# Factor tiles of 128 columns instead of 98 in an agent-attention kernel with an expert pass

## The chip, the cores and the metric

The kernel runs on one core of a Trainium2 chip. The core has TensorE (PE, the matrix array of 128 rows and 128 columns; its weight loads, PEld, run beside its matmuls), VectorE (DVE), ScalarE (ACT), GpSimd (POOL), and DMA queues, of which the one issued by SyncE (SP) carries nearly all of the data. The metric is the device time of one execution in microseconds (us); lower is better. TensorE runs at a granted clock of 2.4 GHz (written 1.00 in the profile) or 1.2 GHz (0.50).

## What is computed

Four batches (B = 4), N = 12608 tokens of C = 128 features, 49 agents for each batch. Agents attend to keys and values, tokens attend to agents, and then the 128 tokens of each batch with the highest gate score go through an expert of two layers with 1024 hidden features:

```
def sm(a, b):
    s = scale * (a @ b.transpose(0, 2, 1))
    s = s - s.max(-1, keepdims=True)
    e = np.exp(s)
    return e / (e.sum(-1, keepdims=True) + 1e-09)
a2k = sm(agents, k)
agent_v = a2k @ v
q2a = sm(q, agents)
out = q2a @ agent_v
# then, for each batch b, with x = out
scores = np.einsum('bsd,d->bs', x, w_gate)
top_idx = np.argpartition(-scores[b], capacity)[:capacity]   # capacity = 128
h = np.maximum(x[b, top_idx] @ w1, 0.0)
out[b, top_idx] = x[b, top_idx] + 1/(1+exp(-scores)) * (h @ w2)
```

## The kernel before, in words

Each batch's tokens are cut into seven chunks, six of 15 tiles and one of 9 tiles of 128 tokens. For each chunk the kernel does the following.

- `k_front` and `q_scores` load a transposed chunk of keys or queries (`xT`) and form the scores `S` with the agents on TensorE; VectorE turns them into tiles `sk` (keys) and `sq` (queries) with the tokens on the partitions, 49 used columns for each tile of tokens.
- `k_exp` and `q_exp` subtract a maximum (GpSimd) and take the exponential (ScalarE).
- `v_tiles` multiplies the key weights with the values into `av` (TensorE, 128 rows by 64 columns of the array, float32); `v_finish` makes of it the float16 matrix `ws` (`d["W"]`), 98 rows, which holds a high and a low half of the agent values, their gate scores, and a column of ones.
- `q_high` and `q_low` write the **factor tile** `f`: for each tile of tokens 98 float16 columns, 49 with the high half of the exponential (ScalarE) and 49 with the low half (GpSimd). The ring of `f` has two buffers (`N_F`).
- `q_turn` transposes `f` on TensorE (98 rows of `fT` in PSUM, eight tiles of tokens in one group) and copies the result to `ft` (ScalarE, a few on VectorE).
- `q_gate` multiplies each transposed tile `ft`, as the weights, with the three gate columns of `ws` (`pg`, 3 moving columns); `q_rates` and `topk` make the scores and the choice of the 128 tokens from it. In `topk` the tile `all` is a broadcast of candidates by TensorE, and VectorE (`ge`) and ScalarE (`ga`) take turns in counting on it.
- `q_out` multiplies each `ft` tile, as the weights, with the high and then the low half of `ws` (`po`, 128 moving columns each); `po` is copied and scaled to `og` by VectorE, ScalarE or ScalarE and GpSimd, and stored.
- `expert` gathers the chosen tokens' queries (`xq`), forms their output again in float32 (`sc`, `e`, `eT`, `xT`, `xe`), and runs the two layers (`ph`, `py`). It runs for batches 0 to 2 together and then for batch 3 alone.

Nothing is issued in the order of the code. A recorder collects all instructions, and a planner (`place`) lays them out once, engine by engine, by hand-set urgencies (`RANKS`), by data dependences, by free buffers, and by a price for each instruction. The price of an instruction counts its columns and the elements of one partition, not the number of partitions. The kernel then issues that order (line 1220), so that each engine works through its own list strictly in sequence. The outputs of batches 1, 3 and 2 (`TAIL`) come late in TensorE's list, with the experts among them.

Of the kernel before, what the change touches and what calls it, by code (L numbers as in the profile page):

```python
# [15 lines left out]
F16 = mybir.dt.float16  # L16
# [4 lines left out]
ALU = mybir.AluOpType  # L21
# [3 lines left out]
P = 128  # L25
# [3 lines left out]
A = 49  # L29
# [4 lines left out]
TMAX = max(CHUNKS)  # L34
# [10 lines left out]
N_F = 2  # L45
# [446 lines left out]
def agent_attention_moe(ctx, tc, qT, kT, va, agT, wgb, w1, w2, consts, qs, outs, capacity):  # L492
    nc = rec = Recorder(tc.nc)
    rec.tag = ("setup", 0)
    B = len(outs)
    C = qT.shape[1]
# [10 lines left out]
    qp = rec.pool(ctx.enter_context(tc.tile_pool(name="qp", bufs=2)), "qp", 2)  # L507
    sm = rec.pool(ctx.enter_context(tc.tile_pool(name="sm", bufs=2)), "sm", 2)
# [35 lines left out]
    def cs(name):  # L544
        return cst[:, spot[name][0]:spot[name][1]]
# [3 lines left out]
    idh = const.tile([P, P], F16, name="idh")  # L549
# [28 lines left out]
    def scores(src, b, c, dst, top=None):  # L578
# [4 lines left out]
        for h in range(2):  # L583
# [85 lines left out]
    def v_finish(b):  # L669
        d = st[b]  # L670
        R = 2 * A
        a = sm.tile([P, C + 1], F32, tag="avs", name=f"avs_{b}", bufs=1)
        nc.vector.tensor_copy(a, d["av"][:, :C + 1])
        pw = psT.tile([P, 512], F32, tag="T", name=f"pw_{b}")
        nc.tensor.matmul(pw[:R, :C + 1], cs("sel"), a, start=True, stop=True)
        yield
        wf = d["wf"] = wfs[:, b]
        rs = sm.tile([R, 1], F32, tag="rs", name=f"rs_{b}", bufs=1)
        nc.vector.tensor_scalar(rs, pw[:R, C:C + 1], 1e-9, None, op0=ALU.add)
        nc.vector.reciprocal(rs, rs)  # L680
# [13 lines left out]
        nc.vector.tensor_scalar(
            iv[:, 1:2].bitcast(I32), iv[:, 0:1].bitcast(I32), -1.0, float((254 + WEXP) << 23),
            op0=ALU.mult, op1=ALU.add,
        )
        up = iv[:R, 1:2]
        ws = sm.tile([R, 3, C + 1], F16, tag="ws", name=f"ws_{b}", bufs=B)
        nc.gpsimd.memset(ws[:, 2, C:], 1.0)  # L700
        nc.vector.tensor_scalar(ws[:, 0, :C], pw[:R, :C], rs, up, op0=ALU.mult, op1=ALU.mult)
        g2 = sm.tile([R, 2], F32, tag="g2", name=f"g2_{b}", bufs=1)
        nc.scalar.mul(g2[:, 0:1], rs, up)
        nc.scalar.mul(g2[:, 1:2], wf[:, C:C + 1], up)
        nc.vector.scalar_tensor_tensor(
            ws[:, 1, :C], pw[:R, :C], g2[:, 0:1], ws[:, 0, :C], op0=ALU.mult, op1=ALU.subtract
        )
        nc.scalar.copy(ws[:, 0, C:], g2[:, 1:2])
        nc.gpsimd.tensor_tensor(ws[:, 1, C:], g2[:, 1:2], ws[:, 0, C:], op=ALU.subtract)
        nc.scalar.mul(iv[:, 0:1], iv[:, 0:1], 2.0 ** -WEXP / FSCALE)  # L710
        d["W"] = ws
        d["iv"] = iv
        yield
# [24 lines left out]
    def q_high(b, c):  # L738
        n = CHUNKS[c]
        d = st[b]  # L740
        sv = d["q", c][:, :n, :A]
        if b in EARLY:
            nc.gpsimd.tensor_tensor(
                sv, sv, d["qm", c][:, :n].unsqueeze(2).broadcast_to([P, n, A]), op=ALU.mult
            )
        f = qp.tile([P, TMAX, 2 * A], F16, tag="f", name=f"f_{b}_{c}", bufs=N_F)
        d["f", c] = f
        copy = {"A": nc.scalar.copy, "P": nc.gpsimd.tensor_copy, "V": nc.vector.tensor_copy}[HI[b]]
        copy(f[:, :n, :A], d["q", c][:, :n, :A])

    def q_low(b, c):
        n = CHUNKS[c]
        f = st[b]["f", c]
        nc.gpsimd.tensor_tensor(
            f[:, :n, A:], st[b]["q", c][:, :n, :A], f[:, :n, :A], op=ALU.subtract
        )

    def q_turn(b, c, t0):
        n = CHUNKS[c]
        d = st[b]  # L760
        nt = min(8, n - t0)
        if nt <= 0:
            return
        f = d["f", c]
        if t0 == 0:
            ring, tag, w = (skp, "sk", TMAX) if b == B - 1 and FT_LAST == "sk" else (ftp, "ft", TMAX)
            if tag == "ft" and c == NCH - 1:
                tag, w = "fs", n
            ft = ring.tile([P, w, AP_], F32, tag=tag, name=f"ft_{b}_{c}", bufs={"sk": N_SK, "ft": N_FT, "fs": B - 1}[tag])
            d["ft", c] = ft.rearrange("p t a -> p (t a)").bitcast(F16)  # L770
        pt = psT.tile([P, 1024], F16, tag="T", name=f"fT_{b}_{c}_{t0}")
        with rec.group():
            for t in range(nt):
                turn = nc.tensor.transpose(pt[:2 * A, P * t:P * t + P], f[:, t0 + t, :], idh)
        if b == B - 1:
            turn.deps.add(d["mb_set"].seq)
        (nc.vector.tensor_copy if TURN[b][t0 // 8] == "V" else nc.scalar.copy)(
            d["ft", c][:2 * A, P * t0:P * (t0 + nt)], pt[:2 * A, :P * nt]
        )

    def q_tile(b, c, t):
        return st[b]["ft", c][:2 * A, P * t:P * t + P]

    def q_gate(b, c):

# [29 lines left out]
    def q_out(b, c, t0):  # L815
# [351 lines left out]
    for b in range(B):  # L1167
# [14 lines left out]
        with rec.at("fin", b):  # L1182
            run(v_finish(b))
        for c in range(NCH):
            with rec.at("q", b, c):
                q_scores(b, c)
            with rec.at("qe", b, c):
                q_exp(b, c)
                q_high(b, c)
                q_low(b, c)  # L1190
            with rec.at("turn", b, c):
                for t0 in range(0, CHUNKS[c], 8):
                    q_turn(b, c, t0)
            with rec.at("gate", b, c):
                q_gate(b, c)
# [103 lines left out]
```

## Time and profile before

| | |
|---|---|
| time, median of 3 runs | 319.38 us (317.65 to 322.01) |
| the profiled execution | 318.6 us |
| its span, first to last instruction | 316.7 us |
| PE busy | 281.7 us, 89% of the span |
| PEld busy | 189.2 us, 60% |
| DVE busy | 225.5 us, 71% |
| POOL busy | 179.9 us, 57% |
| ACT busy | 170.8 us, 54% |
| HBM | 79.87 MB read, 26.21 MB written |
| mean granted clock of TensorE | 0.959 |

The profile comes from one execution. "Busy" is the time in which an engine executes something. PE's matmuls are pipelined, so the durations of neighbouring matmuls overlap; how fast a group of them goes is read from the length of the group, less the length of one, over the number of steps. The granted clock is listed for any stretch of the span. A releaser, "<-DVE og", is what ended an engine's idle time. All times within the span are counted from its first instruction.

### The profile page before, as it was taken

To read this page: it belongs to the slowest core of one execution; us is meant where nothing else is said; L and a number is where in the kernel's file an instruction comes from. 1 tells how busy PE (TensorE), PEld (TensorE's weight loads), DVE (VectorE), ACT (ScalarE), POOL (GpSimd) and SP (SyncE) were. 2 spreads that over 40 slices of the span, in tenths; PEclk is the share of its full clock that TensorE was granted. 3 is DMA by queue.
4 is the path that set the end of the run, shared out by engine and by line. 5 is a ranking of instruction groups with operands and counts; after the bars stand their busy time and mean duration, and the time that the engine had idled before them with its cause. 6 is when DMAs were issued, how large, how long until landed. Compare 5 with 4: busy or idle time off the path is not lost. (4 is left out here: it accounts for less than half of the span.)

```text
span 316.7 us, 8554 instructions
## 1 busy us (share of the span) xinstructions
PE 281.7 (89%) x3524; PEld 189.2 (60%) x3524; DVE 225.5 (71%) x507; ACT 170.8 (54%) x306; POOL 179.9 (57%) x152
## 2 busy tenths in 40 slices
PE   2789879999999999999899998799988969799993
PEld 0133426456335555667664556587978969799593
DVE  0899885797978858658798867848366937769630
ACT  1036645645674533754963666878278835824320
POOL 1046399867869715337723859975245744655232
PEclk9999999999999999999999999999797996958998
DMA  7999999999999999999999997997631893876650
GB/s 291 414 414 419 419 413 416 415 418 418 415 414 407 416 420 332 419 421 386 394 368 402 417 400 281 339 350 210 237 126 58 337 364 128 357 291 261 248 209 31
DMA packets 18203, 106.69 MB, mean 337 GB/s; under 512 B 2032, under 2 KB 3440, under 8 KB 18160
## 3 DMA queue, kind: packets, MB, share of 16 engines
q1 hardware_dynamic: 17472, 105.07, 83.8%
q8 instruction: 30, 0.49, 0.6%
q0 software_dynamic: 256, 0.52, 0.5%
q10 hardware_dynamic: 432, 0.50, 0.4%
q14 instruction: 13, 0.11, 0.1%
HBM read 79.87 MB, written 26.21 MB: 335 GB/s over the span
## 5 line engine op out<-in xcount | busy, mean ns | idle before, releaser
L1220 PE MATMUL S<-xT,ag_sb 128*32 128x480 f32 (+1 forms) x896 | 101.7, 561 | 15.0 <-DMA ag_sb<-agT 6.2
L1220 POOL TENSOR_TENSOR sq<-sq,qm 128x735 f32<-128x735 f32 (+1 forms) x35 | 47.5, 1365 | 54.3 <-DVE qm L1220 51.2
L1220 PEld LDWEIGHTS <-ft 98*128 98x128 f16 x1188 | 65.6, 104 | 15.4 <-issue 13.9
L1220 PE MATMUL po<-ws,ft 98*128 98x128 f16 x792 | 61.9, 236 | 2.8 <-DVE og L1220 1.8
L1220 POOL TENSOR_TENSOR og<-og,r 128x512 f32<-128x512 f32 (+1 forms) x39 | 36.2, 943 | 41.1 <-ACT og L1220 40.9
L1220 PE MATMUL av<-v,sk 128*64 128x129 f32 x792 | 55.5, 283 | 2.8 <-DVE avs L1220 1.3
L1220 PEld LDWEIGHTS S<-xT,ag_sb 128*32 128x32 f32 x896 | 24.0, 110 | 53.9 <-issue 18.8
L1220 PEld LDWEIGHTS av<-v,sk 128*64 128x64 f32 x792 | 47.3, 139 | 14.0 <-issue 6.0
L1220 ACT COPY ft<-fT 98x896 f16<-98x896 f16 (+2 forms) x49 | 43.1, 897 | 23.1 <-PE fT L1220 19.8
L1220 POOL TENSOR_TENSOR f<-sq,f 128x735 f16<-128x735 f32 (+1 forms) x28 | 41.1, 1472 | 19.6 <-ACT f L1220 13.7
L1220 POOL TENSOR_TENSOR sk<-sk,mb 128x735 f32<-128x735 f32 (+1 forms) x28 | 46.8, 1700 | 7.4 <-DVE mb L1220 7.3
L1220 DVE STREAM_TRANSPOSE sq<-S 128x480 f32<-128x480 f32 (+1 forms) x56 | 35.2, 641 | 10.7 <-PE S L1220 10.0
L1220 ACT ACTIVATE sq<-sq,lift 128x735 f32<-128x735 f32 (+1 forms) x28 | 24.6, 887 | 30.1 <-POOL sq L1220 30.1
L1220 DVE TENSOR_REDUCE mx<-S 128x1 f32<-128x480 f32 (+1 forms) x56 | 33.0, 612 | 9.0 <-PE S L1220 8.6
L1220 DVE STREAM_TRANSPOSE sk<-S 128x480 f32<-128x480 f32 (+1 forms) x56 | 34.8, 637 | 4.9 <-PE av L1220 3.1
L1220 PEld LDWEIGHTS <-f 128*98 128x98 f16 x396 | 24.7, 124 | 20.7 <-issue 10.1
L1220 DVE SCALAR_TENSOR_TENSOR ge<-all,top,minus 128x512 bf16<-128x512 f32 x32 | 24.0, 750 | 14.8 <-ACT ga L1220 9.2
L1220 DVE TENSOR_REDUCE qm<-sq 128x15 f32<-128x735 f32 (+1 forms) x35 | 30.3, 867 | 2.4 <-ACT sq L1220 1.6
L1220 PE MATMUL fT<-idh,f 128*98 128x128 f16 x396 | 29.6, 222 | 2.6 <-POOL f L1220 1.0
L1220 DVE TENSOR_TENSOR og<-po,r 128x512 f32<-128x512 f32 (+1 forms) x42 | 26.9, 657 | 5.8 <-PE po L1220 1.9
L1220 ACT ACTIVATE sk<-sk 128x735 f32<-128x735 f32 (+1 forms) x28 | 22.1, 794 | 16.2 <-POOL sk L1220 16.1
L1220 ACT ACTIVATE ga<-all,top 128x512 bf16<-128x512 f32 x32 | 22.0, 687 | 12.2 <-DVE ge L1220 11.5
(130 smaller groups left out, 234.8 us busy)
## 6 DMA issues: line engine op xcount, KB each, us to landing
v<-va SPq DMA_DIRECT2D x24, 967.5 KB, 7.9
xT<-kT SPq DMA_DIRECT2D x24, 960.0 KB, 8.2
xT<-qT SPq DMA_DIRECT2D x24, 960.0 KB, 9.4
out<-og SPq DMA_DIRECT2D x24, 960.0 KB, 4.1
v<-va SPq DMA_DIRECT2D x4, 580.5 KB, 8.5
xT<-kT SPq DMA_DIRECT2D x4, 576.0 KB, 8.4
xT<-qT SPq DMA_DIRECT2D x4, 576.0 KB, 9.7
out<-og SPq DMA_DIRECT2D x4, 576.0 KB
```

Of the source, the lines that this page charges most:

```text
L1220: call(*args, **kwargs)
```

## The change

The factor tiles get 128 columns (`P`) instead of 98 (`2 * A`). The 30 added columns are zero: both buffers of the ring are cleared once, by two GpSimd memsets ahead of the loop, and nothing writes these columns later. The transposes then use 128 columns of the array and give 128 rows of `fT`; the copies to `ft` move 128 partitions; the gates and the outputs use 128 rows as weights. `ws` gets 128 rows as well, whose rows 98 to 127 are cleared by a GpSimd memset for each batch.

```
--- before.py
+++ after.py
@@ -598,6 +598,9 @@
             if top is not None:
                 nc.vector.tensor_reduce(top[:, h:h + 1], ps[:, :w], axis=AX.X, op=ALU.max)
 
+    for i in range(N_F):
+        f = qp.tile([P, TMAX, P], F16, tag="f", name=f"f0_{i}", bufs=N_F)
+        nc.gpsimd.memset(f, 0.0)
     st = [{} for _ in range(B)]
     tail, filled, turns = set(), set(), []
     OUT_PS = ((psO, "O"), (psS, "S"), (psS, "S"), (psS, "S"))
@@ -696,17 +699,18 @@
             op0=ALU.mult, op1=ALU.add,
         )
         up = iv[:R, 1:2]
-        ws = sm.tile([R, 3, C + 1], F16, tag="ws", name=f"ws_{b}", bufs=B)
-        nc.gpsimd.memset(ws[:, 2, C:], 1.0)
-        nc.vector.tensor_scalar(ws[:, 0, :C], pw[:R, :C], rs, up, op0=ALU.mult, op1=ALU.mult)
+        ws = sm.tile([P, 3, C + 1], F16, tag="ws", name=f"ws_{b}", bufs=B)
+        nc.gpsimd.memset(ws[96:], 0.0)
+        nc.gpsimd.memset(ws[:R, 2, C:], 1.0)
+        nc.vector.tensor_scalar(ws[:R, 0, :C], pw[:R, :C], rs, up, op0=ALU.mult, op1=ALU.mult)
         g2 = sm.tile([R, 2], F32, tag="g2", name=f"g2_{b}", bufs=1)
         nc.scalar.mul(g2[:, 0:1], rs, up)
         nc.scalar.mul(g2[:, 1:2], wf[:, C:C + 1], up)
         nc.vector.scalar_tensor_tensor(
-            ws[:, 1, :C], pw[:R, :C], g2[:, 0:1], ws[:, 0, :C], op0=ALU.mult, op1=ALU.subtract
-        )
-        nc.scalar.copy(ws[:, 0, C:], g2[:, 1:2])
-        nc.gpsimd.tensor_tensor(ws[:, 1, C:], g2[:, 1:2], ws[:, 0, C:], op=ALU.subtract)
+            ws[:R, 1, :C], pw[:R, :C], g2[:, 0:1], ws[:R, 0, :C], op0=ALU.mult, op1=ALU.subtract
+        )
+        nc.scalar.copy(ws[:R, 0, C:], g2[:, 1:2])
+        nc.gpsimd.tensor_tensor(ws[:R, 1, C:], g2[:, 1:2], ws[:R, 0, C:], op=ALU.subtract)
         nc.scalar.mul(iv[:, 0:1], iv[:, 0:1], 2.0 ** -WEXP / FSCALE)
         d["W"] = ws
         d["iv"] = iv
@@ -743,7 +747,7 @@
             nc.gpsimd.tensor_tensor(
                 sv, sv, d["qm", c][:, :n].unsqueeze(2).broadcast_to([P, n, A]), op=ALU.mult
             )
-        f = qp.tile([P, TMAX, 2 * A], F16, tag="f", name=f"f_{b}_{c}", bufs=N_F)
+        f = qp.tile([P, TMAX, P], F16, tag="f", name=f"f_{b}_{c}", bufs=N_F)
         d["f", c] = f
         copy = {"A": nc.scalar.copy, "P": nc.gpsimd.tensor_copy, "V": nc.vector.tensor_copy}[HI[b]]
         copy(f[:, :n, :A], d["q", c][:, :n, :A])
@@ -752,7 +756,7 @@
         n = CHUNKS[c]
         f = st[b]["f", c]
         nc.gpsimd.tensor_tensor(
-            f[:, :n, A:], st[b]["q", c][:, :n, :A], f[:, :n, :A], op=ALU.subtract
+            f[:, :n, A:2 * A], st[b]["q", c][:, :n, :A], f[:, :n, :A], op=ALU.subtract
         )
 
     def q_turn(b, c, t0):
@@ -771,15 +775,15 @@
         pt = psT.tile([P, 1024], F16, tag="T", name=f"fT_{b}_{c}_{t0}")
         with rec.group():
             for t in range(nt):
-                turn = nc.tensor.transpose(pt[:2 * A, P * t:P * t + P], f[:, t0 + t, :], idh)
+                turn = nc.tensor.transpose(pt[:, P * t:P * t + P], f[:, t0 + t, :], idh)
         if b == B - 1:
             turn.deps.add(d["mb_set"].seq)
         (nc.vector.tensor_copy if TURN[b][t0 // 8] == "V" else nc.scalar.copy)(
-            d["ft", c][:2 * A, P * t0:P * (t0 + nt)], pt[:2 * A, :P * nt]
+            d["ft", c][:, P * t0:P * (t0 + nt)], pt[:, :P * nt]
         )
 
     def q_tile(b, c, t):
-        return st[b]["ft", c][:2 * A, P * t:P * t + P]
+        return st[b]["ft", c][:, P * t:P * t + P]
 
     def q_gate(b, c):
 
```

GpSimd's list at the start of the program, before (`ws_0` to `ws_3` are the ones of the four batches, `idf` is the float32 identity, of which VectorE makes the float16 identity of the transposes; `sq_2_6` is the queries' last chunk of batch 2, the first real work):

```order
L1220 MEMSET ws_1_290 98x1
L1220 MEMSET ws_2_423 98x1
L1220 MEMSET idf_96 128x128
L1220 MEMSET ws_0_158 98x1
L1220 MEMSET ws_3_556 98x1
L1220 ISA
L1220 AFFINE_SELECT idf_96<-idf_96 128x128
L1220 TENSOR_TENSOR sq_2_6_480<-sq_2_6_480,qm_2_6_484 128x9x49
```

The same place of GpSimd's list now (`f0_0` and `f0_1` are the two buffers of the factor tiles):

```order
L1224 MEMSET ws_1_292 32x387
L1224 MEMSET ws_2_425 32x387
L1224 MEMSET idf_96 128x128
L1224 MEMSET ws_1_292 98x1
L1224 MEMSET ws_2_425 98x1
L1224 MEMSET f0_0_109 128x1920
L1224 MEMSET f0_1_110 128x1920
L1224 ISA
L1224 AFFINE_SELECT idf_96<-idf_96 128x128
L1224 MEMSET ws_0_160 32x387
L1224 MEMSET ws_3_558 32x387
L1224 TENSOR_TENSOR sq_2_6_482<-sq_2_6_482,qm_2_6_486 128x9x49
```

Four of the six added memsets stand ahead of the identity's last step (AFFINE_SELECT), and all six ahead of the first real work. (Two one-column memsets of `ws` that stand before the last row are not shown.)

TensorE's list at the end of the gates of batch 2, before (about 225 to 234 us of the span; `av_3` are the key-value products of batch 3, `all0_2` the broadcast that opens the choice of tokens of batch 2):

```order
L1220 LDWEIGHTS ft_2_1_441
L1220 MATMUL pg_2_434<-ws_2_423,ft_2_1_441 128x3
L1220 MATMUL av_3_543<-v_3_3_546,sk_3_3_520 64x129 x15
L1220 MATMUL av_3_543<-v_3_4_547,sk_3_4_524 64x129 x15
L1220 LDWEIGHTS f_3_6_618
L1220 MATMUL fT_3_6_8_621<-idh_97,f_3_6_618 98x128
L1220 MATMUL all0_2_494<-idf_96,top_2_490 128x128 x4
L1220 MATMUL av_3_543<-v_3_5_548,sk_3_5_528 64x129 x15
```

The same place now:

```order
L1224 LDWEIGHTS ft_2_1_443
L1224 MATMUL pg_2_436<-ws_2_425,ft_2_1_443 128x3
L1224 MATMUL av_3_545<-v_3_3_548,sk_3_3_522 64x129 x15
L1224 MATMUL av_3_545<-v_3_4_549,sk_3_4_526 64x129 x15
L1224 LDWEIGHTS f_3_6_620
L1224 MATMUL fT_3_6_8_623<-idh_97,f_3_6_620 128x128
L1224 MATMUL all0_2_496<-idf_96,top_2_492 128x128 x4
L1224 MATMUL av_3_545<-v_3_5_550,sk_3_5_530 64x129 x15
```

Nothing has moved here; the transpose has 128 output rows instead of 98. The same holds for all of TensorE's, VectorE's, ScalarE's and SyncE's lists: the same instructions in the same order with the same waits, wider where they touch `f`, `fT`, `ft` or `ws`. GpSimd's list differs only at its start.

## Rows read from the trace of the kernel before

**Rows 1.** The page: busy time by engine, and two lines of the 40 slices.

```profile
PE 281.7 (89%) x3524; PEld 189.2 (60%) x3524; DVE 225.5 (71%) x507; ACT 170.8 (54%) x306; POOL 179.9 (57%) x152
PEclk9999999999999999999999999999797996958998
DMA  7999999999999999999999997997631893876650
```

**Rows 2.** Groups by line and shape: busy us, mean ns of one, idle before.

```profile
L1220 PEld LDWEIGHTS <-ft 98*128 98x128 f16 x1188 | 65.6, 104 | 15.4 <-issue 13.9
L1220 PEld LDWEIGHTS <-f 128*98 128x98 f16 x396 | 24.7, 124 | 20.7 <-issue 10.1 <-POOL f L1220 9.0 <-POOL sq L1220 1.6
L1220 PE MATMUL po<-ws,ft 98*128 98x128 f16 x792 | 61.9, 236 | 2.8 <-DVE og L1220 1.8 <-ACT og L1220 0.9
L1220 PE MATMUL fT<-idh,f 128*98 128x128 f16 x396 | 29.6, 222 | 2.6 <-POOL f L1220 1.0 <-POOL sq L1220 0.6 <-DVE m L1220 0.4
L1220 PE MATMUL pg<-ws,ft 98*128 98x3 f16 x396 | 12.3, 167 | 0.3 <-issue 0.3
L1220 POOL TENSOR_TENSOR sk<-sk,mb 128x735 f32<-128x735 f32 x24 | 42.5, 1793 | 7.4 <-DVE mb L1220 7.3
```

**Rows 3.** PE's timeline at full clock: start us, length us, group.

```profile
130.25 1.00 PE L1220 MATMUL fT<-idh,f 128*98 128x128 f16 x15
131.19 0.61 PE L1220 MATMUL po<-ws,ft 98*128 98x128 f16 x8
131.64 0.94 PE L1220 MATMUL pg<-ws,ft 98*128 98x3 f16 x30
232.00 1.97 PE L1220 MATMUL av<-v,sk 128*64 128x129 f32 x30
```

**Rows 4.** Stretches: length, busy us (instructions) by engine, PEclk, DMA share, GB/s.

```profile
222.50:225.90 3.40, 3.40 (x101) 3.38 (x100) 0.04 (x1) 0.93 (x1) 1.25 (x1) 1.00 0.94 295
225.90:229.30 3.40, 3.40 (x34) 3.40 (x34) 2.28 (x8) 0.38 (x1) 0.00 (x0) 0.50 0.56 228
273.70:277.10 3.40, 1.99 (x27) 1.62 (x25) 2.35 (x7) 2.85 (x7) 1.71 (x3) 1.00 1.00 407
277.10:280.50 3.40, 3.02 (x32) 3.01 (x31) 2.54 (x10) 1.08 (x4) 1.98 (x3) 0.50 0.67 276
280.50:287.30 6.80, 6.80 (x61) 6.80 (x60) 4.85 (x15) 2.46 (x5) 4.35 (x5) 0.50 0.87 348
287.30:290.70 3.40, 3.40 (x61) 3.39 (x59) 3.37 (x8) 1.63 (x5) 0.89 (x2) 1.00 0.83 313
```

**Rows 5.** PE's timeline, 223 to 231 us.

```profile
223.67 2.15 PE L1220 MATMUL pg<-ws,ft 98*128 98x3 f16 x75
225.75 5.19 PE L1220 MATMUL av<-v,sk 128*64 128x129 f32 x60
```

**Rows 6.** PE's waits, 236 to 317 us: us in total, times, longest.

```profile
PE all L1220 <- ACT ga L1220: 2.3, 1, 2.3
```

**Rows 7.** PE's timeline, 281 to 290 us.

```profile
281.79 1.46 PE L1220 MATMUL sc<-ag_sb,xT 128*128 128x49 f32 x6
...
283.11 5.96 PE L1220 MATMUL po<-ws,ft 98*128 98x128 f16 x68
288.90 0.49 PE L1220 MATMUL eT<-idf,e 128*49 128x128 f32 x3
```

**Rows 8.** VectorE's timeline at the start of the program.

```profile
9.25 0.23 DVE L1220 CAST tri_b<-cst 128x128 bf16<-128x128 f32 x1 [7.58 <-DMA cst<-consts]
```

**Rows 9.** GpSimd's timeline at the start of the program.

```profile
0.80 0.21 POOL L1220 MEMSET idf<- 128x128 f32 x1
...
1.12 0.29 POOL L1220 TENSOR_SCALAR_AFFINE_SELECT idf<-idf 128x128 f32<-128x128 f32 x1
17.57 0.93 POOL L1220 TENSOR_TENSOR sq<-sq,qm 128x441 f32<-128x441 f32 x1 [16.16 <-DVE qm L1220]
```

**Rows 10.** The chain that ended last: shares of the span by engine and line.

```profile
by line: PE po L1220 4.4%; PE py L1220 2.3%; PE ph L1220 2.0%; PE sc L1220 0.4%; PE xT L1220 0.4%; DVE og L1220 0.4%; PE xe L1220 0.3%; DVE g L1220 0.3%; issue 0.3%; POOL out L1220 0.2%; ACT og L1220 0.2%; POOLq L1225 0.2%; DVE hT L1220 0.1
```

More of the change, by code (lines that the diff above doesn't have):

```diff
@@ L599, in scores @@
                 nc.vector.tensor_reduce(top[:, h:h + 1], ps[:, :w], axis=AX.X, op=ALU.max)
+    for i in range(N_F):
+        f = qp.tile([P, TMAX, P], F16, tag="f", name=f"f0_{i}", bufs=N_F)
+        nc.gpsimd.memset(f, 0.0)
     st = [{} for _ in range(B)]
@@ L698, in v_finish @@
         up = iv[:R, 1:2]
-        ws = sm.tile([R, 3, C + 1], F16, tag="ws", name=f"ws_{b}", bufs=B)
-        nc.gpsimd.memset(ws[:, 2, C:], 1.0)
-        nc.vector.tensor_scalar(ws[:, 0, :C], pw[:R, :C], rs, up, op0=ALU.mult, op1=ALU.mult)
+        ws = sm.tile([P, 3, C + 1], F16, tag="ws", name=f"ws_{b}", bufs=B)
+        nc.gpsimd.memset(ws[96:], 0.0)
+        nc.gpsimd.memset(ws[:R, 2, C:], 1.0)
+        nc.vector.tensor_scalar(ws[:R, 0, :C], pw[:R, :C], rs, up, op0=ALU.mult, op1=ALU.mult)
         g2 = sm.tile([R, 2], F32, tag="g2", name=f"g2_{b}", bufs=1)
@@ L705, in v_finish @@
         nc.vector.scalar_tensor_tensor(
-            ws[:, 1, :C], pw[:R, :C], g2[:, 0:1], ws[:, 0, :C], op0=ALU.mult, op1=ALU.subtract
+            ws[:R, 1, :C], pw[:R, :C], g2[:, 0:1], ws[:R, 0, :C], op0=ALU.mult, op1=ALU.subtract
         )
-        nc.scalar.copy(ws[:, 0, C:], g2[:, 1:2])
-        nc.gpsimd.tensor_tensor(ws[:, 1, C:], g2[:, 1:2], ws[:, 0, C:], op=ALU.subtract)
+        nc.scalar.copy(ws[:R, 0, C:], g2[:, 1:2])
+        nc.gpsimd.tensor_tensor(ws[:R, 1, C:], g2[:, 1:2], ws[:R, 0, C:], op=ALU.subtract)
         nc.scalar.mul(iv[:, 0:1], iv[:, 0:1], 2.0 ** -WEXP / FSCALE)
@@ L745, in q_high @@
             )
-        f = qp.tile([P, TMAX, 2 * A], F16, tag="f", name=f"f_{b}_{c}", bufs=N_F)
+        f = qp.tile([P, TMAX, P], F16, tag="f", name=f"f_{b}_{c}", bufs=N_F)
         d["f", c] = f
@@ L754, in q_low @@
         nc.gpsimd.tensor_tensor(
-            f[:, :n, A:], st[b]["q", c][:, :n, :A], f[:, :n, :A], op=ALU.subtract
+            f[:, :n, A:2 * A], st[b]["q", c][:, :n, :A], f[:, :n, :A], op=ALU.subtract
         )
@@ L773, in q_turn @@
             for t in range(nt):
-                turn = nc.tensor.transpose(pt[:2 * A, P * t:P * t + P], f[:, t0 + t, :], idh)
+                turn = nc.tensor.transpose(pt[:, P * t:P * t + P], f[:, t0 + t, :], idh)
         if b == B - 1:
@@ L777, in q_turn @@
         (nc.vector.tensor_copy if TURN[b][t0 // 8] == "V" else nc.scalar.copy)(
-            d["ft", c][:2 * A, P * t0:P * (t0 + nt)], pt[:2 * A, :P * nt]
+            d["ft", c][:, P * t0:P * (t0 + nt)], pt[:, :P * nt]
         )
     def q_tile(b, c, t):
-        return st[b]["ft", c][:2 * A, P * t:P * t + P]
+        return st[b]["ft", c][:, P * t:P * t + P]
     def q_gate(b, c):
```

## The prediction

> **What bounds the kernel now.** The page is read first [rows 1]. Its two lines of slices show two stages. Up to slice 28 (some 222 us) the DMA engines are busy in seven tenths or more of every slice, nine tenths or more in nearly all, and TensorE's clock is at full rate; after that the DMA digits vary between 0 and 9, and in the same slices the clock falls for the first time (digits down to 5). In the first stage a faster TensorE brings little, since the loads do not come faster. In the second stage the loads are over. There the chain that ended last [rows 10] is followed back from the last instruction, and it lies on TensorE: the outputs po 4.4%, the expert's py 2.3% and ph 2.0%, and only tenths of a per cent on other engines.
>
> Next come the groups by shape, for what the change widens [rows 2]: 396 transposes, 396 gates, 792 outputs, and as many weight loads. Their mean durations (222, 167 and 236 ns) say little, since neighbours overlap. The pace is read from the timeline at full clock [rows 3]: 15 transposes take 1.00 us, so (1.00 − 0.22)/14 = 56 ns a step; 8 outputs (0.61 − 0.24)/7 = 53 ns; 30 gates (0.94 − 0.17)/29 = 27 ns. Gates and outputs load the same weights (98 rows, 128 columns), and the gates show that such a load goes through every 27 ns. So the outputs are paced by their 128 moving columns, not by the load, and the transposes run at the same pace with loads of 98 columns.
>
> Last come stretches of the second stage, for the clock [rows 4]. In 222.5 to 225.9 us TensorE is busy all the time, mostly with 75 gates of 3 moving columns [rows 5], and in the next stretch, to 229.3, the clock is 0.50. In 273.7 to 277.1 it is busy for 1.99 of 3.40 us, and the clock is 0.50 from 277.1 to 287.3, though TensorE is busy for 3.02 of the first 3.40 and for all of the next 6.80 us. At 287.3 it is back at 1.00.
>
> **The change part by part.**
>
> *Transposes, gates, outputs at one clock: 0.* The moving columns are the same (128, 3, 128), and the numbers of instructions too. A step of 56, 27 or 53 ns is set by moving columns or by a load that is already 128 columns wide, and neither changes with the rows. The lower bound is a gain on the 396 loads of f, which become 128 columns wide like those of ft: their means are 124 and 104 ns [rows 2], so at most 396 × 20 ns = 7.9 us if every load were exposed. The steps of 56 ns say that they are covered by the matmul before; I take 0, since even a load of 98 columns fits into the step.
>
> The Trainium skill (TensorE: Matmul & The Clock Gate, section on Fast Weight Load and DoubleRow) says that the fast load is on when the number of weights is 128 and the type is not float32, and that it was measured at about twice the speed. By that page the loads of f become fast: an estimate of 396 × 62 ns = 24.6 us of load time, where the step shows 0 on the path. The same page, in the section on LDWEIGHTS, says that the number of rows of a load does not matter, which would make the padding of ft's rows worth nothing; the gates' 27 ns with 98 rows agree that these loads were fast before.
>
> *Copies of fT to ft: 0.* The elements of one partition stay the same, 1024 or 896; 30 more partitions are moved side by side. ScalarE is at 54% and VectorE at 71% [rows 1].
>
> *Memsets at the start: 0.* The identity's float32 memset writes 128 elements of each partition in 0.21 us [rows 9]. Elements alone would make it 1920/128 × 0.21 = 3.2 us for each factor buffer, an upper estimate since part of the 0.21 is fixed, and 0.6 us for each of the four of 387 elements. Ahead of the identity stand two of each: 7.6 us, hence the identity is there at about 9.0 instead of 1.4 us [rows 9]. VectorE waits for the constants until 9.25 us anyway [rows 8], and GpSimd's first real work starts at 17.57 [rows 9], so the wait for that DMA is the cover. At GpSimd's dearest rate here, 1793 ns for 735 elements [rows 2], the four ahead (4614 elements) would cost 11.3 us, and VectorE would go on at about 12.9 instead of 9.25 us: 3.6 us is the upper bound. I take 0, because a memset reads nothing and the memset's own row is the nearer one.
>
> *The clock in the second stage: −2.8 us.* This is the only place where I see the change reach the path. [Rows 4] show that being busy is not enough for the full clock: TensorE was busy throughout both 222.5 to 225.9 (gates, 3 columns) and most of 277.1 to 283.9 (outputs and small matmuls), and the clock fell or stayed low. So what the array does while it is busy seems to count, and filling 128 instead of 98 rows (gates, outputs) and columns (transposes) makes the same time fuller. No row shows whether rows that hold zeros count; I assume they do.
>
> First place, 225.9 to 229.3 us. The stretch before it holds gates, outputs and transposes, all of which the change widens. At half clock 34 av take 3.40 us; at full clock the step is (1.97 − 0.28)/29 = 58 ns (0.28 us being the last one's own length, an estimate from the outputs' 236 ns and a slightly longer stream) [rows 3], so 34 take 1.97. Gain 1.4 us. Behind av in TensorE's list comes all, which VectorE and ScalarE then count on in turns; TensorE's next all waits 2.3 us for ScalarE's ga [rows 6]. As that wait hangs on the first all, it should move up with it: I take 1.4, bounds 0 and 1.7.
>
> Second place, 280.5 to 287.3 us. If the fuller outputs of 277.1 to 280.5 bring the clock back one stretch sooner, TensorE's 6.80 us become 3.40. But sc stands at its beginning, and eT, which waits for VectorE's and ScalarE's work on sc, behind the 68 outputs [rows 7]. From the end of sc (281.79 + 1.46 = 283.25) to eT (288.90) are 5.65 us, which other engines need. With the full clock sc ends at 280.5 + 2.75/2 = 281.9, so eT can start at 287.5 and not at 288.9: gain 1.4 us. What is late next is TensorE itself: the outputs between end at about 281.9 + 68 × 0.056 = 285.7, so it waits 1.8 us for eT. Bounds: 0, and 6.80 − 4.85 = 1.95 us, as VectorE alone has 4.85 us of work in that stretch [rows 4].
>
> The sum against the profiled execution: 318.6 − 1.4 − 1.4 = 315.8 us. That execution lies 0.8 us below the median of the three runs, 319.4, so the median to expect is 316.6 us.
>
> **The rivals.**
>
> *Nothing changes.* The array's added rows hold zeros, or the clock follows only how long TensorE is busy. For it: 283.11 onward [rows 7], where TensorE ran outputs of 98 rows without a pause, and the clock came back at 287.3. Against it: 222.5 to 225.9, busy without a pause, and then the fall. The time is 318.6, or 319.4 as a median.
>
> The Trainium skill (TensorE: Matmul & The Clock Gate, Part 1, "What's actually happening") says that the clock is set by how busy the PE has been recently, which taken as busy time is this rival; the fall after 225.9 speaks against that reading.
>
> *The clock does not fall at 277.1 either.* TensorE is idle for 1.4 us in the stretch before [rows 4], and the outputs' wider rows would have to outweigh that. Then also the 3.40 us after 277.1 run at full rate, with VectorE's 2.54 as the floor: 0.86 more, and the other places at their upper bounds: 318.6 − 1.7 − 1.95 − 0.86 = 314.1, or 314.9 as a median.
>
> *Slower: the full clock makes a pause that costs it again.* If TensorE must wait 1.8 us for eT, the clock can fall once more right after, where outputs, xT, xe and ph stand on the chain [rows 10]. A stretch of 3.40 us at half clock costs 1.7 us; two in a row cost 3.4, which is more than the 2.8 gained. It decides from the second such stretch on: 318.6 − 2.8 + 3.4 = 319.2, or 320.0; with the gain at the first place absent too, 318.6 − 1.4 + 3.4 = 320.6, or 321.4.
>
> **How the numbers follow.** Forecast (the clock gains at one or both places): 0.52, on its own 315.0 to 318.5. Nothing changes: 0.32, spread like the runs before, 317.65 to 322.01. No fall at 277.1: 0.08. Slower: 0.08. The predicted time is the forecast's, 316.6 us. The range 313.5 to 321.0 takes in the case without a fall at 277.1, the upper bound of the memsets (316.6 + 3.6 = 320.2), nearly all of the runs of "nothing changes", and most of the slower rival. Two per cent (about what a measurement of this kernel can tell from no change) is 6.4 us: faster means below 313.0, slower above 325.8. No case's centre lies beyond either; for runs whose clock falls elsewhere I leave faster 0.08 and slower 0.05, and 0.87 within.
>
> **What would show it.** Right: the steps at full clock stay at 56, 53 and 27 ns; the loads of f get shorter than 124 ns with nothing following from it; the mean granted clock rises above that of before; the av after the last gates of batch 2 run at full clock; the low stretch about 280 us is shorter, and eT starts some 5.6 us after sc ends, with TensorE waiting for it. Wrong: the same low stretches in the same places (then rows of zeros do not count), outputs or transposes whose step at full clock has changed, VectorE's first transpose of S much later than before (the memsets), or a shorter first stage (then TensorE, not the loads, set its pace).

## The result, and the profile after

The changed kernel takes 316.67 us as a median (314.35 to 322.61, 20 runs), the kernel before 319.73 us (316.36 to 322.2, 20 runs). The ratio is 0.9917, with a 95% interval of 0.989 to 0.9945: 1.8 to 3.5 us faster, by less than 2%. The ratios here leave runs out that are far above the fastest of the same kernel; the medians hold all runs. The profiled execution took 316.94 us, with a span of 315.1 us and a mean granted clock of 0.992 (before: 318.6 us, 316.7 us, 0.959).

The page of the changed kernel, the lines that answer to [rows 1]:

```profile
PE 272.8 (87%) x3524; PEld 179.1 (57%) x3524; DVE 226.5 (72%) x507; ACT 170.6 (54%) x306; POOL 186.2 (59%) x158
PEclk9999999999999999999999999999999997999998
DMA  7999999999999999999999999896940695687650
```

TensorE is busy for 9 us less. The clock line has one dip, in slice 33 (counted from 0), where there had been five in slices 28 to 36; the last slices are the end of the program, where TensorE has no work.

The groups by shape, for [rows 2]:

```profile
L1224 PEld LDWEIGHTS <-ft 128*128 128x128 f16 x1188 | 59.7, 98 | 19.9 <-issue 18.4
L1224 PEld LDWEIGHTS <-f 128*128 128x128 f16 x396 | 22.8, 98 | 21.1 <-issue 10.3 <-POOL f L1224 10.1 <-POOL sq L1224 0.8
L1224 PE MATMUL po<-ws,ft 128*128 128x128 f16 x792 | 56.0, 222 | 6.8 <-DVE og L1224 3.7 <-ACT og L1224 3.0
L1224 PE MATMUL fT<-idh,f 128*128 128x128 f16 x396 | 28.8, 220 | 3.0 <-POOL f L1224 1.1 <-ACT ft L1224 1.1 <-DVE m L1224 0.5
L1224 PE MATMUL pg<-ws,ft 128*128 128x3 f16 x396 | 12.2, 167 | 0.2 <-issue 0.2
```

The loads of f went from 124 to 98 ns, and the transposes they feed kept their length (222 before, 220 after). The outputs became 14 ns shorter in the mean, because fewer of them ran at half clock: at full clock 22 of them take 1.40 us in either kernel. What is new is in the last column of po: 6.8 us of waiting for evictions (og), where it was 2.8.

TensorE's timeline of the changed kernel (start, length, group, idle time before it), for [rows 5, 7] and some rows between them:

```profile
225.28 2.14 PE L1224 MATMUL pg<-ws,ft 128*128 128x3 f16 x75
227.35 1.98 PE L1224 MATMUL av<-v,sk 128*64 128x129 f32 x32
230.60 1.76 PE L1224 MATMUL av<-v,sk 128*64 128x129 f32 x28 [1.27 <-issue]
...
232.36 1.11 PE L1224 MATMUL all<-idf,top 128*128 128x128 f32 x8
...
240.01 1.16 PE L1224 MATMUL all<-idf,top 128*128 128x128 f32 x8 [2.34 <-ACT ga L1224]
241.01 1.85 PE L1224 MATMUL po<-ws,ft 128*128 128x128 f16 x30
242.69 0.55 PE L1224 MATMUL fT<-idh,f 128*128 128x128 f16 x7
...
252.93 0.61 PE L1224 MATMUL fT<-idh,f 128*128 128x128 f16 x8 [0.32 <-POOL og L1224]
...
280.56 0.82 PE L1224 MATMUL sc<-ag_sb,xT 128*128 128x49 f32 x6
281.22 0.17 PE L1224 MATMUL pc<-x,p 128*128 128x10 bf16 x1
281.82 3.66 PE L1224 MATMUL po<-ws,ft 128*128 128x128 f16 x60 [0.43 <-DVE og L1224]
286.89 0.61 PE L1224 MATMUL po<-ws,ft 128*128 128x128 f16 x8 [1.41 <-DVE og L1224]
287.34 0.49 PE L1224 MATMUL eT<-idf,e 128*49 128x128 f32 x3
```

The same groups of the kernel before, where they are not among the rows ahead of the prediction:

```profile
238.61 1.26 PE L1220 MATMUL all<-idf,top 128*128 128x128 f32 x8 [2.34 <-ACT ga L1220]
239.67 3.40 PE L1220 MATMUL po<-ws,ft 98*128 98x128 f16 x30
242.87 0.59 PE L1220 MATMUL fT<-idh,f 128*98 128x128 f16 x7
...
251.93 0.61 PE L1220 MATMUL fT<-idh,f 128*98 128x128 f16 x8 [0.32 <-DVE iv L1220]
```

Put side by side, the starts of the same groups show where time went:

| group | before | after | difference | change since the row above |
|---|---|---|---|---|
| gates of batch 2, 75 in a row | 223.67 | 225.28 | +1.61 | |
| first all of batch 2 | 230.96 | 232.36 | +1.40 | −0.2 |
| second all | 238.61 | 240.01 | +1.40 | 0 |
| transposes after it | 242.87 | 242.69 | −0.18 | −1.6 |
| transposes, eight, 9 us later | 251.93 | 252.93 | +1.00 | +1.2 |
| sc | 281.79 | 280.56 | −1.23 | −2.2 |
| eT | 288.90 | 287.34 | −1.56 | −0.3 |

So in this pair the first stage ended 1.6 us later, and the second stage was 3.2 us shorter. Most of the lateness arose at one load: TensorE waits 1.5 us for a chunk of keys, where no such wait stood before.

```profile
147.61 1.01 PE L1224 MATMUL S<-xT,ag_sb 128*32 128x480 f32 x8 [1.49 <-DMA xT<-kT]
```

Stretches of the changed kernel, for [rows 4] (length, busy us by engine, PEclk, DMA share, GB/s):

```profile
222.50:225.90 3.40, 3.40 (x90) 3.40 (x87) 1.02 (x2) 1.59 (x3) 2.43 (x2) 1.00 0.97 225
227.30:230.60 3.30, 2.04 (x37) 1.77 (x34) 2.91 (x10) 1.33 (x3) 0.00 (x0) 1.00 0.62 254
239.50:242.90 3.40, 2.89 (x42) 2.88 (x43) 1.69 (x6) 3.38 (x7) 1.79 (x2) 1.00 0.02 5
262.10:265.60 3.50, 3.50 (x28) 3.44 (x28) 3.04 (x9) 0.87 (x4) 1.83 (x2) 0.51 0.19 77
275.80:279.20 3.40, 2.14 (x34) 1.97 (x33) 2.96 (x9) 2.10 (x6) 2.45 (x3) 1.00 0.72 294
279.20:286.00 6.80, 5.85 (x96) 5.61 (x94) 6.67 (x19) 3.05 (x7) 5.01 (x6) 1.00 0.92 365
```

After the gates the clock stays at 1.00. It stays there too in 275.8 to 286, the place at which it had been 0.50 for ten microseconds. In 279.2 to 286 VectorE is busy for 6.67 of 6.80 us: it is the bound there now, and 2.15 us of this go to one addition, of which more below.

### The profile page after: what moved, and what is told of

The parts are those of the page before. It is cut to its first block, busy times and chain, and to the rows that moved or that the text cites. A ratio compares the mean times of both kernels' runs of the same rounds, so it can differ in the third digit from the quotient of the medians.

```text
span 315.1 us, 8560 instructions
## 1 busy us (share of the span) xinstructions
PE 272.8 (87%) x3524; PEld 179.1 (57%) x3524; DVE 226.5 (72%) x507; ACT 170.6 (54%) x306; POOL 186.2 (59%) x158
## 5 line engine op out<-in xcount | busy, mean ns | idle before, releaser
L1224 PEld LDWEIGHTS <-ft 128*128 128x128 f16 x1188 | 59.7, 98 | 19.9 <-issue 18.4
L1224 PE MATMUL po<-ws,ft 128*128 128x128 f16 x792 | 56.0, 222 | 6.8 <-DVE og L1224 3.7
L1224 PE MATMUL av<-v,sk 128*64 128x129 f32 x792 | 54.2, 277 | 4.0 <-DVE avs L1224 1.3
L1224 ACT COPY ft<-fT 128x896 f16<-128x896 f16 (+2 forms) x49 | 43.0, 895 | 22.1 <-PE fT L1224 19.3
L1224 PEld LDWEIGHTS av<-v,sk 128*64 128x64 f32 x792 | 45.7, 136 | 15.6 <-issue 6.7
L1224 POOL TENSOR_TENSOR f<-sq,f 128x735 f16<-128x735 f32 (+1 forms) x28 | 42.6, 1528 | 19.7 <-ACT f L1224 14.4
L1224 PEld LDWEIGHTS <-f 128*128 128x128 f16 x396 | 22.8, 98 | 21.1 <-issue 10.3
L1224 PE MATMUL fT<-idh,f 128*128 128x128 f16 x396 | 28.8, 220 | 3.0 <-POOL f L1224 1.1
```

The source lines that it names most:

```text
L1224: call(*args, **kwargs)
```

## Experiments

The theory ("rows count"): the granted clock of the second stage follows how much of the array the gates and outputs fill, whatever the added rows hold. Rivals: f's quicker loads; the memory part of the change; only a full array; the data in the rows. Two quantities are read from each profile: the time from the start of the 75 gates of batch 2 to eT, which leaves out the first stage and its loads, and how long the clock stayed low in the stretch that begins at 276 to 281 us.

### The changed kernel again, and the parts of the array that it fills

The control is the changed kernel itself. In the next kernel the transposes stay at 128 columns, and gates and outputs go back to 98 rows; the two after it are made in the same way with `[:112]` (transposes and copies too) and `[:72]` (which leaves out the low half of 26 agents, so its outputs are not the full sums):

```
 def q_tile(b, c, t):
-    return st[b]["ft", c][:, P * t:P * t + P]
+    return st[b]["ft", c][:98, P * t:P * t + P]
...
-    d["pg"][:, STARTS[c] + t, :3], q_tile(b, c, t), d["W"][:, :, C], start=True, stop=True
+    d["pg"][:, STARTS[c] + t, :3], q_tile(b, c, t), d["W"][:98, :, C], start=True, stop=True
...
-    p3[:, t], q_tile(b, c, t0 + t), d["W"][:, i, :C], start=(i == 0), stop=(i == 1)
+    p3[:, t], q_tile(b, c, t0 + t), d["W"][:98, i, :C], start=(i == 0), stop=(i == 1)
```

> The changed kernel again, as the control of this group, beside the kernel before on the same chip. All theories: about 0.990 of the time before, some 316.7 us, mean granted clock about 0.98 against 0.96 before.

> Transposes, copies, memory and memsets as in the changed kernel (128 columns of f, so the quicker loads of f of 98 ns too), but gates and outputs read only rows 0 to 97 again. Theory 'rows count' (the clock follows how many rows the gates and outputs fill): most of the gain is gone, 318.9 us (317.8 to 320), mean clock about 0.965. Rival 'loads' (the gain comes from f's weight loads, 124 to 98 ns): 316.7 us, as the changed kernel. Rival 'memory' (layout or memsets): 316.7 us too.

> One size changed: transposes, copies, gates and outputs use 112 columns and rows, halfway between 98 and 128. Theory 'rows count': between the two kernels, 318 us (317 to 319.2), mean clock about 0.97. Rival 'all rows or none' (only a full array counts): 319.5 us, clock 0.96. Rival 'loads': 316.7 to 317.5 us.

> Gates and outputs read only rows 0 to 71 of the transposed tiles and of ws; this leaves out the low half of 26 of the 49 agents, and nothing else. Instructions, moving columns and order are those of the changed kernel. Theory 'rows count': more stretches of the second stage at 0.50, mean clock below 0.95, and slower than the kernel before: 325 us (321 to 331). Rival 'busy time only' or 'loads': 316.7 to 319.5 us, the clock as in one of the two kernels, since TensorE's time in each instruction is the same.

Measured, on one chip, beside the kernel before (317.38 us, 29 runs, mean clock over them 0.969):

| gates and outputs use | median us (range, runs) | ratio, 95% interval | mean clock over the runs |
|---|---|---|---|
| 128 rows (control) | 318.58 (314.15 to 321.28, 12) | 0.9982 (0.9942 to 1.0023) | 0.983 |
| 112 rows | 318.52 (316.23 to 322.7, 12) | 1.0023 (0.9985 to 1.006) | 0.972 |
| 98 rows, transposes 128 | 320.37 (315.65 to 321.79, 12) | 1.002 (0.9973 to 1.0067) | 0.966 |
| 72 rows | 331.43 (325.6 to 342.31, 6) | none formed | 0.911 |

The clock line of their pages, in the order control, 112 rows, 98 rows, 72 rows:

```profile
PEclk9999999999999999999999999999997995979999
```

```profile
PEclk9999999999999999899999999999977996958998
```

```profile
PEclk9999999999999999999999999999999977857999
```

```profile
PEclk9999999999999999999999999999878956755799
```

The mean clocks over the runs follow the rows, as the theory has it. With 98 rows the clock is 0.018 lower than with 128 (95% interval 0.013 to 0.022), although the transposes, the layout and the memsets are those of the changed kernel; with 72 rows it is lower by far more. So it is the rows of the gates and outputs that count, and not only a full array; which of the two counts more was not separated. The 112 rows lie 0.011 below 128 (0.005 to 0.018) but cannot be told from 98 (0.007 above, with an interval that takes in 0), and their time cannot be told from either neighbour's. Their clock line shows more dips than that of 98 rows; it is from the second longest of their twelve runs (322.43 us, clock 0.954).

With 72 rows the same instructions, in the same order, take longer: the shortest of six runs, 325.60 us, is above the longest of the control's twelve, 321.28. Expected had been 325 (321 to 331); the median is just outside. At full clock nothing has changed (75 gates take 2.14 us, as in the changed kernel), but half clock lasts without a break from 281 to 305 us, although TensorE works without a pause (the stretch, then rows of the timeline):

```profile
281.00:305.00 24.00, 24.00 (x181) 21.85 (x178) 14.15 (x34) 7.00 (x17) 8.20 (x9) 0.50 0.59 238
```

```profile
285.58 7.41 PE L1224 MATMUL po<-ws,ft 72*128 72x128 f16 x68
292.79 0.84 PE L1224 MATMUL eT<-idf,e 128*49 128x128 f32 x3
293.42 4.05 PE L1224 MATMUL po<-ws,ft 72*128 72x128 f16 x36
```

Those 68 outputs take 7.41 us, where the kernel before took 5.96 [rows 7] and the changed one 4.27 (3.66 + 0.61) without its waits. With 128 columns for the transposes alone, f's loads take 98 ns, and there is neither time nor clock to show for it; "loads" falls, and with it the memory part as a cause of the clock.

The control itself missed its expectation: the clock rose as it should (0.983 against 0.969), but the time was not shorter in this group (the interval holds 1), nor is the time of the kernel with 98 rows clearly longer than the control's. Its profile shows why one execution can look so: the gates of batch 2 begin 1.7 us later than in the first profile of the kernel before, and from the gates to eT it saves 1.4 us (63.88 us, against 65.23), which does not cover that. Whether the later start is chance or a cost of the change was the next question.

### Is the first stage late by chance, or by the layout?

The kernel before got a second profile. Another kernel keeps the memory part of the change alone (tiles 128 columns apart, memsets, 128 rows of `ws`), with 98 rows and columns in all instructions; it was run in two groups:

```
-    turn = nc.tensor.transpose(pt[:, P * t:P * t + P], f[:, t0 + t, :], idh)
+    turn = nc.tensor.transpose(pt[:2 * A, P * t:P * t + P], f[:, t0 + t, :2 * A], idh)
...
-    d["ft", c][:, P * t0:P * (t0 + nt)], pt[:, :P * nt]
+    d["ft", c][:2 * A, P * t0:P * (t0 + nt)], pt[:2 * A, :P * nt]
```

(gates and outputs as in the kernel with 98 rows above).

> The kernel before once more, for a second profile of it. All theories: ratio 1.000, mean clock about 0.965. Question: do the last gates of batch 2 (75 in a row) begin at 223.7 us again, as in the first profile, or some 1.5 us later, as in the profiles of the changed kernel (225.3) and of its variants? Theory 'chance of the loads': anywhere from 223.7 to 225.8. Theory 'layout costs the first stage': 223.7 again.

> Only the memory part of the change: f tiles 128 columns apart, all memsets, ws of 128 rows; transposes, copies, gates and outputs use 98 columns and rows as before. Theory 'layout is free': ratio 1.000, clock as before (0.965). Rival 'layout costs the first stage' (GpSimd's subtraction into f takes 1609 instead of 1550 ns in the profiles, or the memsets): ratio 1.004 to 1.006, 1.3 to 2 us slower, with the gates of batch 2 later by as much, and the clock as before.

> Only the memory part of the change again (tiles 128 columns apart and all memsets; engines use 98 columns and rows), since its seven runs scattered over 9 us. Theory 'the wide layout costs the first stage': 1 to 2 us slower than the kernel before. Rival 'layout is free': within 1 us of the kernel before. Both: the stretch from the gates of batch 2 to the end 91 to 93.5 us, clock 0.965.

The kernel before repeated itself: 0.9969 (0.9924 to 1.0014). The memory part gave 321.18 us in seven runs from 314.7 to 323.75 (before: 318.67), ratio 0.9879 (0.9803 to 0.9955), too scattered to say anything, and in the second group 318.01 us in twelve runs (before: 319.01), ratio 0.9969 (0.993 to 1.0009), with a mean clock of 0.968. So layout and memsets are free within what can be measured. The start of the 75 gates in all profiles agrees:

| kernel | gates begin, us |
|---|---|
| before, two profiles | 223.67, 223.25 |
| memory part alone, two | 226.94, 223.28 |
| changed, three | 225.28, 225.42, 225.30 |
| changed, with ones | 222.68 |
| changed, without an addition behind the first stage (below) | 223.84 |
| tiles 98 apart, with and without this addition (below) | 224.88, 223.81 |
| 112, 98 and 72 rows | 225.83, 225.76, 223.82 |

One kernel gives 226.94 and 223.28 in two executions. In the one with 226.94 a load held TensorE up, as in the first two profiles of the changed kernel (the second of them below; the wait of the first, 1.49 us, is shown above):

```profile
138.14 1.93 PE L1224 MATMUL S<-xT,ag_sb 128*32 128x288 f32 x16 [1.84 <-DMA xT<-kT]
```

```profile
148.14 1.01 PE L1224 MATMUL S<-xT,ag_sb 128*32 128x480 f32 x8 [1.74 <-DMA xT<-kT]
```

The loads' chance moves the first stage by up to 3.7 us in one kernel, which is more than the whole gain. The changed kernel's three profiles lie within 0.2 us of each other, 1.6 to 2.2 above the kernel before's two; but up to the S that begins at 121.75 us in the first profile of before, all fourteen profiles lie within 0.6 us of it, with or without the change, and the differences come after it. At the load shown above the third of them waits too, for 0.73 us. The kernels with ones and without the addition have the same first stage and no such wait, and begin their gates at 222.68 and 223.84. A cost of the layout in the first stage does not show; a small one is not excluded.

### Does it matter what the rows hold?

```
-    nc.gpsimd.memset(f, 0.0)
+    nc.gpsimd.memset(f, 1.0)
```

> The changed kernel with ones instead of zeros in the 30 added columns of f (the added rows of ws are zero, so the sums are the same). Theory 'rows count, whatever they hold': same time and same mean clock (0.98) as the changed kernel of the first group, ratio 0.990 to 0.998. Rival 'data counts': a higher clock than the changed kernel, 0.99, and some 1 us faster.

316.76 us (313.7 to 318.5, 12 runs), ratio 0.997 (0.9934 to 1.0006), mean clock over the runs 0.985, against 0.982 and 0.983 for the zeros in the two groups so far: no difference to be told from the zeros. (The interval of the time holds 1, so this group alone does not show a gain over the kernel before; and only f's added columns were changed, the added rows of `ws` stay zero.) In its profile the clock has one dip again:

```profile
PEclk9999999999999999999999999999999997999999
```

### Tiles 98 columns apart

Since no effect of the content shows, a transpose can read its 30 added columns from the next tile, and the tiles need not be spread:

```
-    f = qp.tile([P, TMAX, P], F16, tag="f", name=f"f_{b}_{c}", bufs=N_F)
+    ff = qp.tile([P, TMAX * 2 * A + P - 2 * A], F16, tag="f", name=f"f_{b}_{c}", bufs=N_F)
+    f = d["f", c] = ff[:, :TMAX * 2 * A].rearrange("p (t a) -> p t a", a=2 * A)
...
-    turn = nc.tensor.transpose(pt[:, P * t:P * t + P], f[:, t0 + t, :], idh)
+    turn = nc.tensor.transpose(pt[:, P * t:P * t + P], ff[:, 2 * A * (t0 + t):2 * A * (t0 + t) + P], idh)
```

> The changed kernel again, as the control of this group. Both theories: ratio 0.990 to 0.998 to the kernel before, mean clock 0.983; from the start of the 75 gates of batch 2 to the end 89 to 92 us (93.0 and 91.3 in the two profiles of the kernel before).

> Full rows and columns, but the factor tiles stay 98 columns apart: each transpose reads 128 columns from its tile's start, the last 30 of them the next tile's first 30 (the rows of ws that meet them are zero, so the sums are the same). GpSimd's subtraction into f writes as before the change. Theory 'the wide layout costs the first stage': GpSimd's subtraction is back at 1550 ns, and the kernel is 1 to 2 us faster than the control. Rival 'layout is free, the first stage only scatters': same as the control within 1 us, clock 0.983.

The control now shows the gain again: 316.14 us (313.41 to 319.44) against 319.01, ratio 0.9897 (0.9859 to 0.9934), clock 0.981. Tiles 98 apart give 316.91 us (313.59 to 318.32), 0.9916 (0.988 to 0.9952), clock 0.980: the same. GpSimd's subtraction into f is the one thing in the loop that the spacing does change, in the changed kernel and in this one:

```profile
L1224 POOL TENSOR_TENSOR f<-sq,f 128x735 f16<-128x735 f32 x24 | 38.5, 1609 | 16.3 <-ACT f L1224 11.0 <-issue 3.9 <-POOL f L1224 1.3
```

```profile
L1225 POOL TENSOR_TENSOR f<-sq,f 128x735 f16<-128x735 f32 x24 | 37.1, 1550 | 16.6 <-ACT f L1225 10.1 <-issue 4.9 <-POOL f L1225 1.4
```

59 ns, 24 times, on an engine that is idle for two fifths of its time: it is hidden.

### What the second place waits for now

In the changed kernel's profile VectorE's addition of 1e-9 to three sums stands between sc and eT:

```profile
283.53 0.29 DVE L1224 TENSOR_REDUCE m<-e 128x3 f32<-128x147 f32 x1
283.86 2.15 DVE L1224 TENSOR_SCALAR m<-m 128x3 f32<-128x3 f32 x1
286.04 0.17 DVE L1224 RECIPROCAL m<-m 128x3 f32<-128x3 f32 x1
```

GpSimd's timeline at that time:

```profile
284.14 1.83 POOL L1224 TENSOR_TENSOR og<-og,r 128x512 f32<-128x512 f32 x2
```

The addition begins just before these multiplications and ends 0.04 us after them. In the kernel before it began within the first of them and took 0.7 us less, but ended 0.04 us after the second as well; the addition for batch 3 (one element in each partition), beside which GpSimd does nothing, took 0.15 us:

```profile
285.54 1.83 POOL L1220 TENSOR_TENSOR og<-og,r 128x512 f32<-128x512 f32 x2
285.95 1.45 DVE L1220 TENSOR_SCALAR m<-m 128x3 f32<-128x3 f32 x1
298.35 0.15 DVE L1220 TENSOR_SCALAR m<-m 128x1 f32<-128x1 f32 x1
```

So part of what the clock gained goes into a longer wait on VectorE. The addition was left out, once from the changed kernel and once from the one with tiles 98 apart:

```
-    nc.vector.tensor_scalar(m[:n, 1], m[:n, 1], 1e-9, None, op0=ALU.add)
```

> The changed kernel without the addition of 1e-9 to the experts' sums of exponentials (each sum is at least 1, so float32 gives the same number). In the profile of the changed kernel this addition on VectorE takes 2.15 us for 3 elements, beside two GpSimd multiplications, and eT waits for it. Theory 'the chain from sc to eT sets the second place': that chain gets about 1.9 us shorter, and the kernel 1 to 1.9 us faster than the changed kernel: ratio 0.988 to 0.993. Rival 'whatever VectorE does next waits in its place' (the reciprocal): same as the changed kernel, and the reciprocal takes about 2 us.

> The kernel with tiles 98 columns apart, and without the addition of 1e-9 to the experts' sums. If the two gains add up: 1.5 to 2 us faster than the one with the addition, ratio 0.983 to 0.989 to the kernel before; the stretch from the gates to the end 88 to 90 us.

VectorE's rows without it, and GpSimd's multiplications there:

```profile
283.81 0.30 DVE L1223 TENSOR_REDUCE m<-e 128x3 f32<-128x147 f32 x1
284.14 0.18 DVE L1223 RECIPROCAL m<-m 128x3 f32<-128x3 f32 x1
284.42 1.83 POOL L1223 TENSOR_TENSOR og<-og,r 128x512 f32<-128x512 f32 x2
```

The reciprocal, which now begins as long before the multiplications as the addition had, does not wait for them: it ends before they begin. (So it is not shown that a reciprocal beside them would go through.) From sc to eT it is 5.20 us (280.85 to 286.05) instead of 6.78, 1.6 us less where 1.9 were expected. The times: 315.84 us (313.42 to 316.46, six runs), ratio 0.9872 (0.9818 to 0.9925), beside the kernel with ones in the same group at 0.997, and 315.05 us (313.71 to 318.14, six runs), 0.9887 (0.983 to 0.9944), beside the kernel with tiles 98 apart and the addition at 0.9916. The chain is shorter, as expected; that the whole kernel is faster than the changed one by it is likely by the medians, but the intervals overlap, so it isn't shown.

## Why the prediction came out

**The time** was met: 316.67 us for 316.6, inside 313.5 to 321.0, and within 2%. The cause was met too, and the sum only as a whole. Of its two terms the first gave nothing and the second more than forecast, and the first stage of this pair was late by about as much as the first term was to save. That the median lies within 0.1 us of the forecast is in good part luck: by their ratios the three groups saved about 2.7, 0.6 and 3.3 us, where 2.8 were forecast. The range says little by itself, since it takes in nearly all of "nothing changes"; the clock and the timeline decide.

**Work at one clock, 0:** right. In the timeline of the changed kernel 30 outputs at full clock take 1.85 us, (1.85 − 0.22)/29 = 56 ns a step, and 75 gates 2.14 us, 27 ns. The 53 ns for outputs in the prediction came from taking off a mean of 236 ns that holds outputs at half clock; with 0.22 us its row gives 56 as well. f's quicker loads gave nothing, as the kernel with 128 columns for the transposes alone showed.

By the Trainium skill (TensorE: Matmul & The Clock Gate, section on Fast Weight Load and DoubleRow) f's loads were to become fast with 128 columns, about twice as fast. The direction agrees: they went from 124 to 98 ns, the length that ft's loads have in the first stage with 98 or 128 rows (97 and 98 ns). The listed length did not halve, and it was worth nothing because the loads were covered.

**Memsets and copies, 0:** right for the path, and the copies kept their length (1010 and 1008 ns for 1024 elements on ScalarE). The four memsets ahead delayed the identity more than the old list did, but not up to the DMA's end at 9.27 us:

```profile
1.79 3.34 POOL L1224 MEMSET f<- 128x1920 f16 x2
5.17 0.29 POOL L1224 TENSOR_SCALAR_AFFINE_SELECT idf<-idf 128x128 f32<-128x128 f32 x1
```

The memsets of f took 1.67 us each, half of my upper estimate of 3.2.

**First place, −1.4 forecast, −0.2 measured:** the clock did stay at 1.00, and 32 av took 1.98 us, where 34 had taken 3.40 [rows 4]. But then TensorE sat idle for 1.27 us ahead of the next av (the trace names no releaser). At half clock the av had been late enough for that wait not to appear. The step that failed was to let the whole gain pass on to all: I looked at what comes behind av, not at what the later av themselves wait for. Nor is this fall a fixture: of the five profiles with 98 rows only the first has it. The second profile of the kernel before shows the same cover with 98 rows and full clock:

```profile
225.33 1.98 PE L1220 MATMUL av<-v,sk 128*64 128x129 f32 x32
228.84 1.76 PE L1220 MATMUL av<-v,sk 128*64 128x129 f32 x28 [1.53 <-issue]
```

There it takes 7.38 us from the gates to all, in the other three without the fall 7.10 to 7.54, and 7.29 in the one with it. So the fall at this place had cost nothing, and there was nothing to gain. The rest of the reading held: from all to the second all it is 7.65 us before and after.

**Not foreseen, −1.6 and then +1.2:** in 239.5 to 242.9 the clock had been 0.50 before and was 1.00 after; 30 outputs took 1.85 instead of 3.40 us. Most of that was given back in the next ten microseconds, more than half of it in waits of outputs for ScalarE's og. In the two later profiles of the changed kernel (controls) this dip is back, and in three profiles with 98 rows (the second of before, the first of the memory part, transposes alone) it is absent, so it depends on the execution.

**Second place, −1.4 forecast, −2.3 measured** (from the outputs at 272.87 to eT it is 16.03 us before, from the same at 273.62 after 13.72; a dip at 262 us that is 3.4 us shorter gave 0.2 more). The mechanism was right: the clock was back early, TensorE then waited, and the time from sc to eT stayed nearly what other engines need (7.11 before, 6.78 after). TensorE's wait is 0.43 and 1.41 us, as much as the 1.8 forecast, but not for eT: it is ahead of the outputs in between, for evictions (og) on VectorE, the longer one behind the addition. What I had as a rival of 0.08, that the clock would not fall at 277 at all, is what happened here and in two more profiles with 128 rows, and it is why the term was too small. In the second profile of the changed kernel and with tiles 98 apart the clock falls for 3.4 us, as the forecast had it, and the same stretch takes 14.82 and 14.76 us, 1.2 and 1.3 less than in the first profile before (the second, where the clock was low for 6.8 us only, has 14.88). Over all profiles the length of the low stretch at this place tells 98 from 128 rows without an overlap; the time from the gates to eT does so only in the main:

| gates and outputs use | low stretch from 276 to 281 us on, us | gates to eT, us |
|---|---|---|
| 72 rows | 23.9 | 68.97 |
| 98 rows (before twice, memory part twice, transposes alone) | 10.2, 6.8, 13.7, 10.2, 13.7 | 65.23, 63.36, 65.52, 65.27, 65.48 |
| 112 rows | 10.2 | 66.93 |
| 128 rows (changed three times, ones, tiles 98 apart) | 0, 3.4, 0, 0, 3.4 | 62.05, 63.88, 63.30, 61.33, 63.40 |
| 128 rows without the addition (tiles 128 and 98 apart) | 3.4, 0 | 62.22, 60.46 |

The 66.93 us of 112 rows are not from the clock alone: some 2 us of them arise ahead of the second all, where that profile takes 16.98 us from the gates and the first of before 14.94.

From eT to the end it is 27.8 to 28.1 us in every profile but the one with 72 rows (32.5): the slower rival, a new fall in the experts' stretch, never came about, and no gain was made there either.

**Nothing changes** is refuted for the clock. For the time it stays true in one of three groups, where the ratio of the changed kernel was 0.998 (0.994 to 1.002); the other two gave 0.992 and 0.990. The loads' chance in the first stage is as large as the effect, and the group without a gain ran on another chip than the two groups after it; what of this made the difference is open.

The Trainium skill (TensorE: Matmul & The Clock Gate, Part 1, "What's actually happening") says that the clock is set by how busy the PE has been. Taken as time spent in matmuls, that does not agree with these runs: the same instructions in the same order got 0.91 with 72 rows and 0.98 with 128.

## What to carry to other kernels

Where TensorE's clock falls in a stretch with narrow matmuls or pauses, see how many rows of the array the matmuls use: filling them up, with whatever the other operand's zeros cancel, costs no time in the matmuls themselves. (Wider transposes alone gave nothing here.) Price the gain by the engine that comes next: here TensorE was busy for 8.9 us less, and the second stage became 3.2 us shorter, since the rest turned into waits, the largest part of them for evictions. A fall of the clock costs nothing where TensorE would have waited right behind it anyway, as at the first place. And when the effect is smaller than the scatter of another stage, measure it from a marker behind that stage.

## What the runs showed of the hardware that was not expected

- The clock follows the rows that gates and outputs use: means over the runs of 0.911, 0.966 to 0.971 and 0.980 to 0.985 for 72, 98 and 128 rows (112 rows, 0.972, cannot be told from 98); ones or zeros in the added rows make no difference that shows (0.985 and 0.983).
- An addition to three elements on VectorE took 1.45 or 2.15 us beside two GpSimd multiplications in SBUF, and ended 0.03 to 0.04 us after the second in all twelve profiles that have it; with GpSimd idle one to a single element took 0.15 us. No run separates the cause.
- GpSimd's float16 output took 1609 instead of 1550 ns for 735 elements when its tiles lay 128 instead of 98 columns apart.
